# The rebiased weight word goes to a PSUM bank: a three-step weight unpacking in front of a split-precision MLP

## The chip, the cores and the metric

The kernel runs on one core of a Trainium2 chip. The metric is device time in microseconds, taken as the median over repeated executions. A core has TensorE (PE in the profile; PEld is its weight load), VectorE (DVE), ScalarE (ACT), GpSimd (POOL) and SyncE (SP, which issues most of the transfers). They share an SBUF; matmuls write to PSUM, which this kernel uses as eight banks of 128 x 512 words.

## The reference

```python
# q, k, v: [4, 8, 576, 64]; up-local attention, factor 4
q_d, k_d, v_d = (t.reshape(B, H, 144, 4, D).mean(axis=3) for t in (q, k, v))
out_up = np.repeat(sm_attn(q_d, k_d, v_d), 4, axis=2)       # pooled attention
mask = np.abs(pos[:, None] - pos[None, :]) < 4              # band of 7 keys
scores = np.where(mask, scale * q @ k.T, -1e9)
out_local = softmax(scores) @ v
x = (out_up + out_local).transpose(0, 2, 1, 3).reshape(2304, 512)
h = x @ w_in;  x = (h - np.tanh(h)) @ w_out                 # first MLP, 512 -> 2048 -> 512
h = x @ w_in2; return (h * np.cos(h)) @ w_out2              # second MLP
```

The weights come as float64, so the kernel reads each as two 32-bit words.

## The kernel before, in words

**Chunks.** The tokens go through the first MLP in six chunks: batch 0 (512 columns), two halves of batch 1 (256 columns each, the second and the third chunk), batch 2, batch 3 (512 each), and the remaining rows of all batches (256). While one chunk is in the MLP, the attention of the next ones is worked out. After that the second MLP runs.

**Attention.** The band of seven keys is computed by products on POOL (`prod_s` L551 for scores, `prod_v` L600 for values, 128 x 896 each) and sums on DVE (L556, L604), with the softmax between them. The pooled attention uses TensorE (scores `pa_s`, transposes `pa_t`, values `pa_v`). `fin_t` transposes the result into a PSUM tile `pa_x`, `fin_add` adds the pooled part (L642) and makes the high half `xh` (ACT), and `fin_lo` makes the low half `xl` (L653, DVE). A chunk's first-layer matmuls (L742) need `xh` and `xl` of all four head pairs.

**The first MLP.** Every product is computed as three matmuls of high and low halves: wh·xh, wh·xl, wl·xh. L742 is the first layer; ACT's tanh and DVE's L786 make g = h - tanh h, which ACT (L753) and DVE (L788) split into `gh` and `gl`; L762 is the second layer, into four accumulators.

**The weights.** Class `Weights` brings the 32 tiles of one MLP (128 x 512 each, 16 of w_in called `i`, 16 of w_out called `o`) into halves. `load` fetches the two words into a tile `raw` (SP). `begin` runs two ACT instructions: L120 rebiases the exponent of the high word from `raw` into a tile `wf`, L122 prepares the low word inside `raw`. `mid` merges the two on DVE (L126: shift `wf` left by three, or with the word in `raw`, back into `wf`), and makes the high half `hi` from `wf` (L132 on POOL for the first three tiles, ACT L134 for the others). `end` makes the low half (L141 on POOL, `wf` minus `hi`). `tick` does, for one tile, `mid`, the `load` of a later one into the `raw` that came free, the `begin` of the next tile, and the `end` of the one before. SP issues its transfers in one row: the loads of `raw`, and those of `qt`, `kt`, `vt` for the attention.

**What sets the order.** Up to program time 41 (about 48 us in the trace) the instructions run as they are written. Behind that, a scheduler orders them by its own simulated timeline and by priorities; the written times (`add_events`, `pos`) only say when work is offered. Each engine then runs its instructions strictly in its row. PSUM has two banks called `h` (pool `ps_h`, hidden layer), two called `a` (`ps_a`, everything that the attention puts into PSUM), and four others, which are the attention's (`ps_1`, `ps_w`) at first and the accumulators' from program time 41.

Of the kernel before, what the change touches and what calls it, by code (L numbers as in the profile page):

```python
# [8 lines left out]
F32 = mybir.dt.float32  # L9
F32R = mybir.dt.float32r  # L10
AF = mybir.ActivationFunctionType
# [16 lines left out]
def kernel(  # L28
# [11 lines left out]
    nc = tc.nc  # L40
# [15 lines left out]
    U32, U16 = mybir.dt.uint32, mybir.dt.uint16  # L56
    PS = bass.MemoryType.PSUM

    def pool(name, bufs=1, **kw):
        return tc.tile_pool(name=name, bufs=bufs, **kw)  # L60
# [5 lines left out]
    ps_h = ctx.enter_context(pool("ps_h", 2, space=PS))  # L66
    ps_a = ctx.enter_context(pool("ps_a", 2, space=PS))
# [9 lines left out]
    wts_b = []  # L77
# [4 lines left out]
    class Weights:  # L82
# [27 lines left out]
        def begin(self):  # L110
            if self.begun == len(self.order):
                return
            r2, = self.tmp[self.begun]
            wd = wst.tile([128, 512], F32, tag="wf", name="wf", bufs=3)
            r4 = r2.rearrange("p c w -> p (c w)").bitcast(U16).rearrange("p (c w) -> p c w", w=4)
            self.tmp[self.begun] += [wd, r4]
            self.begun += 1


            nc.scalar.activation(wd, r2[:, :, 1].bitcast(F32), AF.Prelu, scale=2.0 ** -112, alpha=-2.0 ** 32)  # L120

            nc.scalar.activation(r2[:, :, 0], r4[:, :, 1], AF.Copy, scale=2.0 ** -13, bias=-0.5 + 2.0 ** -14)  # L122

        def mid(self):
            r2, wd, r4 = self.tmp[self.mids]
            nc.vector.scalar_tensor_tensor(out=wd.bitcast(U32), in0=wd.bitcast(U32), scalar=3, in1=r2[:, :, 0],  # L126
                                           op0=ALU.logical_shift_left, op1=ALU.bitwise_or)
            kind, f = self.order[self.mids]
            pl = w2e if self is W2 and self.mids < NE else wts if f < KA else wts_b[0]
            hi, lo = pl.tile([128, 2, 512], F32R, tag=f"{kind}{f}", name=f"{kind}{f}").rearrange("p a c -> a p c")  # L130
            if self is W1 and self.mids < 3:
                nc.gpsimd.tensor_copy(hi, wd)  # L132
            else:
                nc.scalar.activation(hi, wd, AF.Copy)  # L134
            self.hi[kind, f], self.lo[kind, f] = hi, lo
            self.mids += 1

        def end(self, eng):
            r2, wd, r4 = self.tmp.pop(self.done)
            kind, f = self.order[self.done]  # L140
            eng.tensor_tensor(out=self.lo[kind, f], in0=wd, in1=self.hi[kind, f].bitcast(F32), op=ALU.subtract)  # L141
            self.done += 1

        def tick(self, rawp, eng):

            if self.done == len(self.order):
                return
            if self.mids < len(self.order):
                if self.begun == self.mids:
                    self.begin()  # L150
                self.mid()
                self.load(rawp)
                if self.begun < self.loaded:
                    self.begin()
            if self.mids > self.done + 1 or self.mids == len(self.order):
                self.end(eng)
# [651 lines left out]
    W1, W2 = Weights(w_in1, w_out1), Weights(w_in2, w_out2)  # L808
# [169 lines left out]
```

## Time and profile before

| | |
|---|---|
| median of 3 executions | 949.79 us (948.58 to 951.3) |
| profiled execution, span from first to last instruction | 946.1 us |
| mean granted TensorE clock in it | 0.983 |
| busy share of the span: PE, PEld, DVE, ACT, POOL | 96%, 79%, 64%, 51%, 44% |
| chain that ended last, by engine | PE 68%, DVE 12%, ACT 6%, DMA 5%, POOL 4% |

The span is that of one profiled execution. The median lies 3.7 us above it; that is taken for what lies around a span in an execution. Times in rows are microseconds from the start of the span. The busy shares are averages over stages that differ much: the attention ends early, the second MLP has PE almost alone.

### The profile page before, as it was taken

To read this page: it belongs to the slowest core of one execution; us is meant where nothing else is said; L and a number is where in the kernel's file an instruction comes from. 1 tells how busy PE (TensorE), PEld (TensorE's weight loads), DVE (VectorE), ACT (ScalarE), POOL (GpSimd) and SP (SyncE) were. 2 spreads that over 40 slices of the span, in tenths; PEclk is the share of its full clock that TensorE was granted. 3 is DMA by queue.
4 is the path that set the end of the run, shared out by engine and by line. 5 is a ranking of instruction groups with operands and counts; after the bars stand their busy time and mean duration, and the time that the engine had idled before them with its cause. 6 is when DMAs were issued, how large, how long until landed. Compare 5 with 4: busy or idle time off the path is not lost.

```text
span 946.1 us, 13554 instructions
## 1 busy us (share of the span) xinstructions
PE 904.2 (96%) x4930; PEld 747.6 (79%) x4930; DVE 602.0 (64%) x964; ACT 479.3 (51%) x1012; POOL 413.7 (44%) x432
## 2 busy tenths in 40 slices
PE   7869989999998999999999989999999999999995
PEld 4547757899997777778889968888888888888894
DVE  6599898899989873762236486545645553654453
ACT  3559767333433343383238886445544453544453
POOL 3578988889888983630005543111111110111110
PEclk9978989999999999999999999999999999999998
DMA  9688635532322222181024631010101010100100
GB/s 180 127 287 283 196 113 165 161 99 82 103 85 92 82 66 63 55 254 37 1 89 138 216 114 45 1 45 1 45 1 45 5 41 0 45 23 1 45 1 23
DMA packets 65819, 81.73 MB, mean 86 GB/s; under 512 B 21846, under 2 KB 46428, under 8 KB 65752
## 3 DMA queue, kind: packets, MB, share of 16 engines
q1 hardware_dynamic: 64520, 76.14, 27.0%
q0 software_dynamic: 1232, 4.72, 1.5%
q8 instruction: 39, 0.64, 0.3%
q14 instruction: 28, 0.23, 0.1%
HBM read 71.40 MB, written 9.44 MB: 85 GB/s over the span
## 4 chain that ended last, share of the span: by engine, by line
PE 68%; DVE 12%; ACT 6%; DMA 5%; POOL 4%; issue 3%; SPq 0%; ACTq 0%; DVEq 0%; POOLq 0%
PE h L742 32%; PE oacc L899 21%; PE acc L762 12%; DVE wf L126 3%; DMA raw<-in_moe_w_out_dram 2%; POOL pr L600 2%; DVE s L556 1%; DMA raw<-in_moe_w_in_dram 1%; DMA vt<-in_v_dram 1%; POOL pr L551 1%; ACT raw L122 1%; DMA qt<-in_q_dram 1%; ACT wf L120 1%; DVE h L786 1%; DVE o L604 1%
## 5 line engine op out<-in xcount | busy, mean ns | idle before, releaser
L899 PE MATMUL oacc<-o,i 128*128 128x512 f32 x864 | 209.8, 392 | 3.3 <-ACT i L749 2.8
L742 PE MATMUL h<-xh,i 128*128 128x512 f32 (+1 forms) x768 | 207.7, 346 | 4.2 <-DVE gl L788 4.2
L762 PE MATMUL acc<-gh,o 128*128 128x512 f32 (+1 forms) x768 | 197.9, 339 | 5.7 <-ACT gh L753 5.6
L742 PE MATMUL h<-x2h,i 128*128 128x512 f32 (+1 forms) x640 | 193.2, 369 | 0.0
L899 PEld LDWEIGHTS oacc<-o,i 128*128 128x128 f32 x864 | 160.8, 188 | 39.2 <-ACT i L749 4.0
L914 POOL TENSOR_SCALAR y<-y 128x512 f32<-128x512 f32 (+1 forms) x80 | 47.4, 593 | 327.5 <-ACT y L912 322.2
L742 PEld LDWEIGHTS h<-xh,i 128*128 128x128 f32 x768 | 137.0, 194 | 22.2 <-DVE gl L788 4.9
L762 PEld LDWEIGHTS acc<-gh,o 128*128 128x128 f32 x768 | 132.7, 190 | 23.3 <-ACT gh L753 7.7
L742 PE MATMUL h<-xl,i 128*128 128x512 f32 (+1 forms) x384 | 133.3, 348 | 3.8 <-DVE xl L500 2.8
L742 PEld LDWEIGHTS h<-x2h,i 128*128 128x128 f32 x640 | 116.8, 188 | 21.7
L551 POOL TENSOR_TENSOR pr<-qt,kt 128x896 f32<-128x896 f32 x56 | 120.8, 2171 | 28.1 <-DVE o L604 19.4
L762 PE MATMUL acc<-gl,o 128*128 128x512 f32 (+1 forms) x384 | 129.1, 339 | 0.0
L742 PE MATMUL h<-x2l,i 128*128 128x512 f32 (+1 forms) x320 | 117.9, 369 | 0.0
L600 POOL TENSOR_TENSOR pr<-vt,s 128x896 f32<-128x896 f32 x56 | 107.4, 1964 | 4.1 <-issue 1.7
L919 DVE TENSOR_TENSOR h<-h,rr 128x512 f32<-128x512 f32 (+1 forms) x80 | 51.6, 645 | 83.3 <-ACT rr L918 83.1
L917 ACT ACTIVATE rr<-rr 128x512 f32<-128x512 f32 (+1 forms) x80 | 47.1, 589 | 103.4 <-DVE rr L916 103.4
L742 PEld LDWEIGHTS h<-xl,i 128*128 128x128 f32 x384 | 74.5, 194 | 12.6 <-DVE xl L500 3.5
L921 DVE TENSOR_TENSOR i<-h,i 128x512 fp32r<-128x512 f32 (+1 forms) x80 | 50.6, 634 | 48.7 <-ACT i L749 48.5
L762 PEld LDWEIGHTS acc<-gl,o 128*128 128x128 f32 x384 | 72.8, 190 | 8.2 <-issue 0.4
L126 DVE SCALAR_TENSOR_TENSOR wf<-wf,raw 128x512 uint32<-128x512 uint32 x64 | 64.4, 1015 | 21.7 <-ACT wf L120 15.1
L785 ACT ACTIVATE th<-h 128x512 f32<-128x512 f32 x72 | 42.7, 594 | 67.8 <-PE h L742 67.7
L753 ACT ACTIVATE gh<-h 128x512 fp32r<-128x512 f32 x72 | 42.8, 595 | 65.9 <-PE acc L762 45.1
(184 smaller groups left out, 1264.9 us busy)
## 6 DMA issues: line engine op xcount, KB each, us to landing
raw<-in_moe_w_in_dram SPq DMA_DIRECT2D x32, 512.0 KB
raw<-in_moe_w_out_dram SPq DMA_DIRECT2D x32, 512.0 KB
kt<-in_k_dram SPq DMA_DIRECT2D x16, 320.0 KB
vt<-in_v_dram SPq DMA_DIRECT2D x16, 320.0 KB
out_dram<-os SPq DMA_DIRECT2D x18, 256.0 KB
kt<-in_k_dram SPq DMA_DIRECT2D x16, 256.0 KB
vt<-in_v_dram SPq DMA_DIRECT2D x16, 256.0 KB
x2l<-x2d POOLq DMA_DIRECT2D x4, 1024.0 KB, 5.7
```

Of the source, the lines that this page charges most:

```text
L126: nc.vector.scalar_tensor_tensor(out=wd.bitcast(U32), in0=wd.bitcast(U32), scalar=3, in1=r2[:, :, 0], op0=ALU.logical_shift_left, op1=ALU. ...
L551: nc.gpsimd.tensor_tensor(out=pr.rearrange("p j f d -> p j (f d)"), in0=view(L["q", h], [[0, OFF], [1, 2 * D]], off=f * D), in1=view(L["k" ...
L600: nc.gpsimd.tensor_tensor(out=pr.rearrange("p f d j -> p j f d"), in0=view(L["v", h], [[D, OFF], [D, 2], [1, D]], off=f * D), in1=view(L[" ...
L742: nc.tensor.matmul(hp[:, i * n:i * n + n], lhsT=wt[:, kk * 128:(kk + 1) * 128], rhs=xt, start=(c == 0), stop=(c == 3 * KD - 1))
L753: nc.scalar.activation(gh, hp, AF.Copy)
L762: nc.tensor.matmul(acc[e], lhsT=wt[:, e * 128:(e + 1) * 128], rhs=gt, start=(f == 0 and i == 0), stop=(f == KF - 1 and i == 2))
L785: it = nc.scalar.activation(th, hp, AF.Tanh)
L899: nc.tensor.matmul(acc[t], lhsT=gt[:, t * 128:(t + 1) * 128], rhs=wt, start=(g == 0 and a_ == 0), stop=(g == KF - 1 and a_ == 2))
L914: ip = nc.gpsimd.tensor_scalar(out=y, in0=y, scalar1=-ROUND, scalar2=-TWO_PI_HI, op0=ALU.add, op1=ALU.mult)
L917: nc.scalar.activation(r, r, AF.Abs)
L919: nc.vector.tensor_tensor(out=hp, in0=hp, in1=r, op=ALU.mult)
L921: nc.vector.tensor_tensor(out=G[f][1], in0=hp, in1=G[f][0].bitcast(F32), op=ALU.subtract)
```

## The change

For the first MLP, `begin` writes the rebiased word no longer to `wf` but to a PSUM tile `wp`. It takes this tile from the rotation `h` for the tiles unpacked up to program time 41 (six of them), and from the rotation `a` for the other 26. The merge reads `wp` and `raw` and writes `wf`. The step that begins the next tile right behind a merge is dropped for the first MLP, so that a tile is begun in the step that merges it. The second MLP's weights are unpacked as before. From here on the changed program's lines stand four lower than the same lines of before (L126 is L130, L653 is L657).

```diff
@@ def begin(self):
             wd = wst.tile([128, 512], F32, tag="wf", name="wf", bufs=3)
             r4 = r2.rearrange("p c w -> p (c w)").bitcast(U16).rearrange("p (c w) -> p c w", w=4)
-            self.tmp[self.begun] += [wd, r4]
+            pre = wd
+            if self is W1:
+                bank = (ps_a, "a") if wts_b else (ps_h, "h")
+                pre = bank[0].tile([128, 512], F32, tag=bank[1], name="wp")
+            self.tmp[self.begun] += [wd, r4, pre]
             self.begun += 1
-            nc.scalar.activation(wd, r2[:, :, 1].bitcast(F32), AF.Prelu, scale=2.0 ** -112, alpha=-2.0 ** 32)
+            nc.scalar.activation(pre, r2[:, :, 1].bitcast(F32), AF.Prelu, scale=2.0 ** -112, alpha=-2.0 ** 32)
             nc.scalar.activation(r2[:, :, 0], r4[:, :, 1], AF.Copy, scale=2.0 ** -13, bias=-0.5 + 2.0 ** -14)
@@ def mid(self):
-            r2, wd, r4 = self.tmp[self.mids]
-            nc.vector.scalar_tensor_tensor(out=wd.bitcast(U32), in0=wd.bitcast(U32), scalar=3, in1=r2[:, :, 0],
+            r2, wd, r4, pre = self.tmp[self.mids]
+            nc.vector.scalar_tensor_tensor(out=wd.bitcast(U32), in0=pre.bitcast(U32), scalar=3, in1=r2[:, :, 0],
                                            op0=ALU.logical_shift_left, op1=ALU.bitwise_or)
@@ def tick(self, rawp, eng):
                 self.mid()
                 self.load(rawp)
-                if self.begun < self.loaded:
+                if self.begun < self.loaded and self is not W1:
                     self.begin()
```

How the rows move is seen at two places. The first is ACT's row at the first weight tiles, in the part that runs as written. Before, the second tile (L120 and L122) is begun right behind the first:

```order
L120 ACTIVATE wf_627<-raw_214 128x512
L122 ACTIVATE raw_214<-raw_214 128x512
L120 ACTIVATE wf_635<-raw_216 128x512
L122 ACTIVATE raw_216<-raw_216 128x512
L302 ACTIVATE pt_642<-pa_t_638 128x320
L480 ACTIVATE cp_645<-cpt_646 70x512
L325 ACTIVATE up0_131<-pa_v_664 128x128
L326 ACTIVATE up_l2_99<-pa_v_664 128x32
L311 ACTIVATE pe_554<-pa_t2_678 16x320
```

Now the same place on ACT reads so, in the changed program's lines:

```order
L124 ACTIVATE wp_628<-raw_214 128x512
L126 ACTIVATE raw_214<-raw_214 128x512
L306 ACTIVATE pt_640<-pa_t_636 128x320
L484 ACTIVATE cp_643<-cpt_644 70x512
L329 ACTIVATE up0_131<-pa_v_662 128x128
L330 ACTIVATE up_l2_99<-pa_v_662 128x32
L315 ACTIVATE pe_554<-pa_t2_676 16x320
L124 ACTIVATE wp_683<-raw_216 128x512
L126 ACTIVATE raw_216<-raw_216 128x512
```

The second tile's two instructions went behind five of the attention.

The second place is DVE's row where chunk 0's last hidden tile is done and the second chunk's input is finished. `xl` here is the second chunk's, `pa_x` and `up` its transposed result and its pooled part; L604 sums value products of the third chunk, and L556 score products of batch 2. Before:

```order
L788 TENSOR_TENSOR gl_2079<-h_2062,gh_2078 128x512
L604 TENSOR_REDUCE o_1967<-pr_1968 128x2x64
L642 TENSOR_TENSOR pa_x_2120<-pa_x_2120,up_1751 128x256
L604 TENSOR_REDUCE o_1967<-pr_1988 128x2x64
L642 TENSOR_TENSOR pa_x_2123<-pa_x_2123,up_1939 128x256
L588 RECIPROCAL r_1963<-r_1963 128x4
L653 TENSOR_TENSOR xl_2102<-pa_x_2120,xh_2101 128x256
L625 TENSOR_REDUCE vd_2438<-vt_2199 128x64
L653 TENSOR_TENSOR xl_2102<-pa_x_2123,xh_2101 128x256
L604 TENSOR_REDUCE o_2011<-pr_2012 128x2x64
```

Now, from the first score sum of batch 2 (L560) to the second chunk's last `xl` (L657):

```order
L560 TENSOR_REDUCE s_2228<-pr_2229 128x7x2
L646 TENSOR_TENSOR pa_x_2126<-pa_x_2126,up_1240 128x256
L560 TENSOR_REDUCE s_2228<-pr_2237 128x7x2
L657 TENSOR_TENSOR xl_2134<-pa_x_2126,xh_2133 128x256
...
L560 TENSOR_REDUCE s_2228<-pr_2244 128x7x2
...
L560 TENSOR_REDUCE s_2228<-pr_2283 128x7x2
L657 TENSOR_TENSOR xl_2134<-pa_x_2152,xh_2133 128x256
L646 TENSOR_TENSOR pa_x_2155<-pa_x_2155,up_1971 128x256
L560 TENSOR_REDUCE s_2286<-pr_2287 128x7x2
L570 TENSOR_REDUCE m_2294<-s_2228 128x8
L657 TENSOR_TENSOR xl_2134<-pa_x_2155,xh_2133 128x256
```

Before, the last `xl` of the second chunk stood ahead of every score sum of batch 2; now it stands behind five of them. POOL's row has its products in the same order as before.

## Rows read from the trace of the kernel before

**Rows 1.** The page's part 1: busy time of each engine over the span.

```profile
PE 904.2 (96%) x4930; PEld 747.6 (79%) x4930; DVE 602.0 (64%) x964; ACT 479.3 (51%) x1012; POOL 413.7 (44%) x432
```

**Rows 2.** Stretches: length; busy (count) PE, PEld, DVE, ACT, POOL; clock; DMA share, GB/s.

```profile
120.00:130.00 10.00, 6.96 (x29) 4.80 (x27) 9.82 (x12) 7.61 (x20) 8.33 (x10) 0.94 0.27 85
130.00:140.00 10.00, 10.00 (x39) 6.93 (x38) 8.81 (x8) 6.35 (x12) 9.86 (x6) 0.72 0.32 96
60.00:160.00 100.00, 90.48 (x395) 69.12 (x391) 91.11 (x124) 77.08 (x177) 91.90 (x80) 0.88 0.65 210
...
192.00:300.00 108.00, 106.98 (x850) 101.22 (x851) 97.54 (x152) 42.33 (x118) 94.16 (x78) 1.00 0.30 92
```

**Rows 3.** The merge L126, 40 to 165 us: shortest, median, longest (ns).

```profile
L126 DVE SCALAR_TENSOR_TENSOR wf<-wf,raw x32: 675/1210/2607, 44.3 to 156.4; 128x512 uint32<-128x512 uint32 x32
```

**Rows 4.** The hidden layer's L788 on DVE, same stretch, same columns.

```profile
L788 DVE TENSOR_TENSOR gl<-h,gh x13: 654/678/692, 80.4 to 160.5; 128x512 fp32r<-128x512 f32 x13
```

**Rows 5.** Groups by shape, 60 to 160 us: busy us, mean ns | idle before.

```profile
L126 DVE SCALAR_TENSOR_TENSOR wf<-wf,raw 128x512 uint32<-128x512 uint32 x28 | 35.6, 1282 | 2.6 <-ACT wf L120 2.5
...
L551 POOL TENSOR_TENSOR pr<-qt,kt 128x896 f32<-128x896 f32 x12 | 27.6, 2306 | 1.9 <-DMA kt<-in_k_dram 1.3 <-DVE s L556 0.5
L141 POOL TENSOR_TENSOR o<-wf,o 128x512 fp32r<-128x512 f32 x16 | 22.4, 1405 | 1.0 <-ACT o L134 1.0
L141 POOL TENSOR_TENSOR i<-wf,i 128x512 fp32r<-128x512 f32 x13 | 18.4, 1414 | 1.8 <-ACT i L134 1.6
L600 POOL TENSOR_TENSOR pr<-vt,s 128x896 f32<-128x896 f32 x8 | 16.8, 2134 | 0.1
L560 POOL TENSOR_TENSOR s<-s,mask_t 128x28 f32<-128x28 f32 x6 | 3.2, 532 | 2.4 <-DVE s L556 2.4
L260 POOL COPY qz<-klq 64x64 f32<-64x64 f32 x8 | 2.8, 351 | 0.2
```

**Rows 6.** POOL groups by shape, 190 to 300 us, where no merge runs.

```profile
L551 POOL TENSOR_TENSOR pr<-qt,kt 128x896 f32<-128x896 f32 x25 | 52.7, 2125 | 5.4 <-DVE s L556 3.3 <-DVE o L604 1.8 <-DVE pr__2362 L279 0.2
L600 POOL TENSOR_TENSOR pr<-vt,s 128x896 f32<-128x896 f32 x20 | 37.3, 1929 | 0.4 <-DVE s L556 0.2
L260 POOL COPY qz<-klq 64x64 f32<-64x64 f32 x8 | 1.9, 233 | 0.3
L560 POOL TENSOR_TENSOR s<-s,mask_t 128x56 f32<-128x56 f32 x6 | 1.9, 309 | 2.7 <-DVE s L556 2.7
```

**Rows 7.** Timeline around one merge, DVE: start, duration, instruction.

```profile
115.33 1.92 DVE L126 SCALAR_TENSOR_TENSOR wf<-wf,raw 128x512 uint32<-128x512 uint32 x1
```

**Rows 8.** Timeline there, POOL.

```profile
116.67 1.74 POOL L141 TENSOR_TENSOR i<-wf,i 128x512 fp32r<-128x512 f32 x1
...
118.80 1.29 POOL L141 TENSOR_TENSOR o<-wf,o 128x512 fp32r<-128x512 f32 x1
```

**Rows 9.** DVE's timeline, 176 to 200 us, [idle before <- releaser].

```profile
185.40 0.41 DVE L653 TENSOR_TENSOR xl<-pa_x,xh 128x256 fp32r<-128x256 f32 x1
...
199.91 1.07 DVE L556 TENSOR_REDUCE s<-pr 128x14 f32<-128x896 f32 x1
```

**Rows 10.** POOL's timeline, 176 to 204 us.

```profile
191.56 0.52 POOL L260 COPY qz<-klq 64x64 f32<-64x64 f32 x2
...
197.36 2.13 POOL L551 TENSOR_TENSOR pr<-qt,kt 128x896 f32<-128x896 f32 x1 [0.65 <-DVE s L556]
```

**Rows 11.** PE's timeline around the second chunk's start.

```profile
185.87 0.39 PE L742 MATMUL h<-xl,i 128*128 128x256 f32 x1 [0.82 <-DVE xl L653]
...
190.96 0.73 PE L762 MATMUL acc<-gh,o 128*128 128x256 f32 x4 [0.74 <-ACT gh L753]
```

**Rows 12.** PE's timeline where batch 2 follows.

```profile
303.33 0.50 PE L742 MATMUL h<-xh,i 128*128 128x512 f32 x1 [2.29 <-DVE gl L788]
```

**Rows 13.** Timeline of DVE and SP at the second tile.

```profile
46.17 0.68 DVE L126 SCALAR_TENSOR_TENSOR wf<-wf,raw 128x512 uint32<-128x512 uint32 x1
...
46.88 0.35 SPq L108 DMA_DIRECT2D raw<-in_moe_w_out_dram  x1
```

More of the change, by code (lines that the diff above doesn't have):

```diff
@@ L138, in end @@
         def end(self, eng):
-            r2, wd, r4 = self.tmp.pop(self.done)
+            r2, wd, r4, pre = self.tmp.pop(self.done)
             kind, f = self.order[self.done]
```

## Prediction

> **What bounds the kernel now.** The page's busy shares come first [rows 1]: PE is busy 904.2 us of 946.1, so on the whole the time is PE's, and only two things can change it, PE's idle time and PE's clock. The stretches say where those are [rows 2]. From 192 us on PE is busy in 106.98 of 108 us at full clock: there nothing helps, and whatever shift reaches that point is carried to the end. From 60 to 160 us three engines are nearly full at once: PE 90.48 us of 100, DVE 91.11, POOL 91.90. [...] So the weights' stage, 60 to 160 us, and its handover to the second chunk decide.
>
> Next I look at what the merge costs. Its groups by shape and its spread [rows 3, 5] show 675 ns at the shortest, 1210 at the median and 2607 at the longest, 35.6 us in 28 merges. Another DVE operation of the same size in the same stretch, L788, which reads one operand from PSUM, keeps to 654 to 692 ns in all 13 cases [rows 4]. So the stretch is not hard on DVE as such; it is hard on the operation with both inputs in SBUF. POOL pays as well: the `lo` subtraction that ran beside a merge of 1.92 us took 1.74 us, and the next one, without a merge beside it for most of its length, 1.29 [rows 7, 8].
>
> The handover is the last place to look. The second chunk's last `xl` starts on DVE at 185.40 and takes 0.41 us [rows 9]; PE waits 0.82 us for it at 185.87 [rows 11]. It is the gate of that chunk.
>
> **The change, part by part.** *The merge.* With one operand in PSUM it has the operand places of L788, so I take 0.68 us for it in place of 1282 ns: 28 × 0.60 = 17 us of DVE time come free. The bounds are 0.68 (L788) and 1.28 (no effect). DVE is no bound of its own here, since it stands in turn with POOL; so this does not go into the sum directly. What goes in is what POOL gets.
>
> [...]
>
> *POOL.* I compare group means of 60 to 160 us with those of 190 to 300 us, where no merge runs [rows 5, 6]. Score products: 12 × (2306 - 2125) ns = 2.2 us. Value products: 8 × (2134 - 1929) = 1.6. The `lo` subtractions, against the 1.29 us of one almost alone [rows 8]: 16 × 0.115 + 13 × 0.124 = 3.4. L560: 6 × (532 - 309) = 1.3, where 309 ns is for twice as many elements. L260: 8 × 0.118 = 0.9. About 13 other small operations and two products before 60 us I put at 1.6 by the same proportions (an estimate). Together 11.0 us. At most POOL would gain the merge's whole uncontended length each time, 28 × 0.675 = 19 us; at least nothing.
>
> POOL's 8 us of idle in that stretch [rows 2] are partly waits for DVE (2.4 for L556 [rows 5]) and can shrink when DVE is ahead: I take 2, between 0 and 5.
>
> *The later beginning.* A tile is now begun in its merging step. In the written part the second tile's pair on ACT stands behind five of the attention's instructions, and its merge, 46.17 us before, is that much later; SP's next weight load waits for the `raw` that this merge frees (46.88) [rows 13], and the loads of `qt` and `kt`, POOL's first food, are queued behind it. I charge 1 us (0 to 2, the length of the inserted instructions). Later on each merge waits for its own tile's two ACT instructions; ACT has 23 us of 100 free [rows 2], so I count nothing for it, and price the case that this cover fails as a rival. ACT's write to PSUM shows in no row. It would have to be 0.7 us longer per tile to use up ACT's free 23 us on 32 tiles; I take nothing for it.
>
> So POOL's lane is ahead by S = 11 + 2 - 1 = 12 us at the handover (9 to 16 for this case).
>
> *The handover.* The order shows the thing that speaks against a gain. The second chunk's last `xl` now stands behind five score sums of batch 2 on DVE. DVE runs its row strictly, so the gate is no longer where the second chunk's own transposes are ready, but where POOL has made five more products of 2.1 us. In the times of before, the fifth product starts at 197.36 [rows 10], its sum at 199.91, and after 1.07 us of that sum, an estimated 0.2 for the short maximum behind it and 0.41 for the `xl`, the gate opens at 201.6. The copies, which stand between those products before (0.52 us at 191.56 [rows 10]), stand earlier now, and idles as the 0.65 before the fifth shrink: less 1.6 with their small neighbours, that is 200. With S = 12 the gate opens at 188.0 against 185.8 before: **+2.2 us** (184 to 191, so -1.8 to +5.2).
>
> *PE beside it.* Up to there PE has the same work as before, and gets its weights earlier; what it saves before the gate it loses in front of it as one long idle piece. After 3 us of idle, the stretch of before paid (1 - 0.72) × 10 = 2.8 us at the lower clock [rows 2]. I take **+3** (0 if its waits are split by other matmuls, 3.4 if the lower level lasts as long again). The 0.74 us for `gh` that follow in the second chunk [rows 11] lie behind other work when the two chunks stand closer together: **-1**. The wait of 2.29 us at batch 2's beginning [rows 12] gets a little shorter since POOL and DVE enter it earlier: **-1** (0 to -3.3).
>
> The sum is 2.2 + 3 - 1 - 1 = **+3.2 us**. From 946.1 the span comes to 949.3; with the 3.7 us by which the median lies above the profiled span the time is **953.0 us**.
>
> **The rivals.** *A, the forecast*: the merge is freed, but the handover waits for the five products. For it speaks the order, which is certain, and POOL's load of 91.90 of 100. Own range 949.5 to 956.5 from S of 16 to 9.
>
> *B, faster*: POOL's lane gains so much that the gate opens before PE has its own work done. That takes S above about 16. For it: in that stretch DVE and POOL wait for one another, and a lane gains more than its parts when both get shorter. If S is 20 (19 by the upper bound, 2 regained, 1 lost) the gate opens at 180, and PE is the bound: of its 9.5 us of idle and about 3 of lower clock before that point I give back half, 6, and 1 at batch 2, so 939.1 of span and 942.8 us. Range 939 to 946.9. [...]
>
> *C, slower by more*: two banks `a` carry the attention's PSUM traffic, and 26 tiles now use them too. Each `wp` holds one from ACT's write to the merge's end, some 2 us at least with 0.7 of merge, that is over 50 us of the 200 bank-microseconds of the stretch. Pooled transposes wait for a bank, or DVE stands at a merge whose tile is not begun, and the sums behind it wait. If 7 of the 12 us are lost so, S is 5, the gate opens at 195, and +9.2 + 1 gives 960 (957 to 963 for S of 8 to 2).
>
> *D, the merge is not freed*: the contention goes with something else than the operand's place. S is then 1, the gate opens at 199, +13.2 + 1, and the time is 964. L788's steady 678 ns beside the same POOL operations speak against it.
>
> **How the numbers follow.** A 0.50, B 0.30, C 0.15, D 0.05. Within 0.3%, or 2.85 us, of before (about what a measurement of this kernel can tell from no change) is up to 952.6; nearly half of A lies below that, 0.24. Slower is the rest of A with C and D, 0.46; faster is B, 0.30. Since cases of both signs hold much, the range reaches from inside B to inside C, 941.5 to 961.5, which leaves out about 0.09 below and 0.09 above.
>
> **What would show it.** Right: merges at 0.68 us throughout; L551 at 2.13 and L141 at 1.29 us in 60 to 160 us; POOL's products reaching batch 2 some 12 us earlier; PE idle in front of a first-layer matmul with `xl` as releaser near 188 us, and a lower granted clock behind it. Wrong: merges still above 1 us (D), idle on DVE before L130 or PE waits for banks `a` that add up to more than 5 us (C), or a second chunk that starts before 182 us without a wait for `xl` (B).

## The result and the profile after

The changed kernel takes 963.53 us (961.46 to 965.18, 4 runs) against 949.53 us for the one before: a ratio of 1.0143, with a 95% interval from 1.0124 to 1.0161. It is 14.0 us slower. The prediction had the side right, but its 953.0 us (941.5 to 961.5) lies short of it, and so does the upper end of the range. The profiled execution has a span of 963.3 us, 17.2 more than that of before. Against their own medians the two profiled executions differ by 3 us (0.2 and 3.4 below), so 3 of the 17.2 are differences between executions. Part of them stands at the very start: the first weight tile's ACT instruction, ahead of which the two rows are the same, is at 44.79 us in the changed kernel's trace and at 43.04 in that of before.

The merges first: one instruction's spread over 40 to 175 us, as [rows 3].

```profile
L130 DVE SCALAR_TENSOR_TENSOR wf<-wp,raw x32: 653/682/692, 46.0 to 155.7; 128x512 uint32<-128x512 uint32 x32
```

All 32 run in 653 to 692 ns. The same groups by shape as [rows 5], 60 to 160 us:

```profile
L130 DVE SCALAR_TENSOR_TENSOR wf<-wp,raw 128x512 uint32<-128x512 uint32 x29 | 19.5, 682 | 10.0 <-ACT wp L124 5.0 <-POOL i L145 2.9 <-POOL o L145 1.5
...
L555 POOL TENSOR_TENSOR pr<-qt,kt 128x896 f32<-128x896 f32 x13 | 27.6, 2123 | 0.0
L145 POOL TENSOR_TENSOR o<-wf,o 128x512 fp32r<-128x512 f32 x16 | 20.8, 1298 | 4.2 <-ACT o L138 4.1
L145 POOL TENSOR_TENSOR i<-wf,i 128x512 fp32r<-128x512 f32 x14 | 18.2, 1300 | 0.6 <-ACT i L138 0.4
L604 POOL TENSOR_TENSOR pr<-vt,s 128x896 f32<-128x896 f32 x9 | 17.3, 1954 | 0.1
L564 POOL TENSOR_TENSOR s<-s,mask_t 128x28 f32<-128x28 f32 x7 | 1.8, 254 | 5.9 <-DVE s L560 5.9
L264 POOL COPY qz<-klq 64x64 f32<-64x64 f32 x6 | 1.4, 238 | 0.2
```

POOL's score products take 2123 ns and its `lo` subtractions 1298 and 1300: what they take where no merge runs [rows 6, 8]. The relief is whole. But POOL now idles 5.9 us in one piece for a score sum and 4.1 for `hi` halves, and DVE 10.0 us in front of merges, where it was 2.6 [rows 5]. The start shows where the lateness begins. SP's timeline, in the stretch of [rows 13]:

```profile
50.98 0.35 SPq L108 DMA_DIRECT2D raw<-in_moe_w_out_dram  x1
51.39 0.43 SPq L221 DMA_DIRECT2D qt<-in_q_dram  x1
```

The weight load that stood at 46.88 stands at 50.98, and the load of `qt` behind it. POOL's first product of the third chunk follows at 57.88, where it began at 53.22 before:

```profile
57.88 2.09 POOL L555 TENSOR_TENSOR pr<-qt,kt 128x896 f32<-128x896 f32 x1
```

Rows of ACT say what stood in front of the second tile's pair:

```profile
44.79 0.61 ACT L124 ACTIVATE wp<-raw 128x512 f32<-128x512 f32 x1
...
47.95 0.28 ACT L329 ACTIVATE up<-pa_v 128x128 f32<-128x128 f32 x1 [1.16 <-PE pa_v L326]
...
49.02 0.60 ACT L124 ACTIVATE wp<-raw 128x512 f32<-128x512 f32 x1
```

The first two tiles in the kernel before:

```profile
43.04 0.65 ACT L120 ACTIVATE wf<-raw 128x512 f32<-128x512 f32 x1
...
44.15 0.66 ACT L120 ACTIVATE wf<-raw 128x512 f32<-128x512 f32 x1
```

Of the five instructions, two wait for PE (1.16 us, and 0.38 at the other). The second tile is begun 4.2 us behind the first, where it was 1.1: 3.1 us later. It adds up from tile to tile: the sixth is begun 26.5 us behind the first (at 71.30), where it was 18.4 (at 61.46). PE's timeline shows what that becomes, and the far end of the stage:

```profile
71.55 0.76 PE L746 MATMUL h<-xh,i 128*128 128x512 f32 x1 [6.92 <-ACT xh L500]
...
115.83 0.38 PE L634 MATMUL pa_qk<-ident,qkd 128*128 128x128 f32 x2
...
180.13 0.39 PE L766 MATMUL acc<-gh,o 128*128 128x512 f32 x1
184.58 1.12 PE L298 MATMUL pa_t<-ident,pe 128*128 128x128 f32 x4 [4.06 <-ACT pe L292]
...
202.55 0.74 PE L766 MATMUL acc<-gh,o 128*128 128x256 f32 x4 [1.12 <-ACT gh L757]
204.80 0.55 PE L746 MATMUL h<-xh,i 128*128 128x256 f32 x1 [1.51 <-DVE gl L792]
```

The same places in the kernel before, which were not among its rows shown above:

```profile
64.50 1.23 PE L742 MATMUL h<-xh,i 128*128 128x512 f32 x2
...
80.88 0.68 PE L630 MATMUL pa_qk<-ident,qkd 128*128 128x128 f32 x2
...
182.34 0.39 PE L762 MATMUL acc<-gh,o 128*128 128x512 f32 x1
```

Chunk 0 starts 7 us later and yet ends 2.2 us earlier, so the stage in between gave back 9. (In the trace of the run g3 below, whose rows are the same up to there, chunk 0 starts at 68.98, so of the 7 us some 2.6 can be a difference between executions.) Then PE stands still for 4.06 us and waits for the pooled attention of the second chunk's last head pair, whose transposes (`pa_t`) were done near 155 us before. The second pair's pooled steps began at 115.83 us in place of 80.88. The gate, on POOL and on DVE, as [rows 9, 10]:

```profile
184.36 10.27 POOL L555 TENSOR_TENSOR pr<-qt,kt 128x896 f32<-128x896 f32 x5
```

```profile
195.01 1.08 DVE L560 TENSOR_REDUCE s<-pr 128x14 f32<-128x896 f32 x1
196.00 0.26 DVE L570 TENSOR_REDUCE m<-s 128x8 f32<-128x56 f32 x1
196.17 0.42 DVE L657 TENSOR_TENSOR xl<-pa_x,xh 128x256 fp32r<-128x256 f32 x1
```

The last low half follows the fifth score sum without a gap, at 196.17 instead of 185.40: 10.8 us later. Stretches, with the columns of [rows 2]:

```profile
60.00:70.00 10.00, 4.16 (x61) 3.30 (x58) 6.46 (x12) 3.71 (x7) 6.52 (x4) 0.50 0.33 103
...
180.00:190.00 10.00, 5.23 (x24) 2.52 (x22) 7.56 (x14) 5.20 (x17) 9.65 (x8) 0.69 0.65 215
190.00:200.00 10.00, 8.45 (x49) 8.17 (x49) 9.74 (x18) 2.53 (x8) 10.00 (x8) 0.63 0.42 130
200.00:210.00 10.00, 7.37 (x49) 6.99 (x49) 9.46 (x17) 4.79 (x15) 8.41 (x12) 0.83 0.26 79
...
310.00:337.00 27.00, 23.81 (x105) 18.40 (x104) 21.39 (x35) 10.29 (x28) 22.51 (x21) 0.94 0.23 63
```

PE's granted clock is 0.69, 0.63 and 0.83 of full clock in the three stretches from 180 to 210 us. The second chunk's first wait of its second layer stands 11.6 us later (202.55), the next wait 12.8 (204.80 for 192.01 before), and batch 2's wait of [rows 12] 13.4 (316.75 for 303.33). The remaining 3.8 of the profile's 17.2 us are behind that, partly in lower clock, as the 0.94 from 310 to 337 us (1.00 before, from 297 to 324).

### The profile page after: what moved, and what is told of

Read it like the earlier page. It is cut to its first block, busy times and chain, and to the rows that moved or that the text cites. A ratio compares the mean times of both kernels' runs of the same rounds, so it can differ in the third digit from the quotient of the medians.

```text
span 963.3 us, 13558 instructions
## 1 busy us (share of the span) xinstructions
PE 910.1 (94%) x4922; PEld 753.9 (78%) x4930; DVE 584.0 (61%) x964; ACT 479.2 (50%) x1012; POOL 401.2 (42%) x432
## 3 DMA queue, kind: packets, MB, share of 16 engines
q1 hardware_dynamic: 64520, 76.14, 26.5%
## 4 chain that ended last, share of the span: by engine, by line
PE 71%; DVE 8%; DMA 8%; ACT 5%; POOL 5%; issue 2%; SPq 0%; ACTq 0%; DVEq 0%; POOLq 0%
PE h L746 33%; PE oacc L903 20%; PE acc L766 13%; DMA raw<-in_moe_w_out_dram 3%; DMA raw<-in_moe_w_in_dram 2%; POOL pr L555 2%; POOL pr L604 2%; DVE wf L130 1%; DMA kt<-in_k_dram 1%; ACT raw L126 1%; PE idle L361 1%; DVE s L560 1%; PE pa_s L271 1%; ACT i L138 1%; PE pa_t L298 1%
## 5 line engine op out<-in xcount | busy, mean ns | idle before, releaser
L746 PE MATMUL h<-xh,i 128*128 128x512 f32 (+1 forms) x768 | 209.9, 349 | 11.0 <-ACT xh L500 6.9
L746 PEld LDWEIGHTS h<-xh,i 128*128 128x128 f32 x768 | 139.4, 198 | 29.9 <-issue 9.8
L555 POOL TENSOR_TENSOR pr<-qt,kt 128x896 f32<-128x896 f32 x56 | 117.9, 2120 | 38.9 <-DVE o L608 33.3
L604 POOL TENSOR_TENSOR pr<-vt,s 128x896 f32<-128x896 f32 x56 | 105.8, 1932 | 6.3 <-DVE o L608 4.3
L790 DVE TENSOR_TENSOR h<-h,th 128x512 f32<-128x512 f32 x72 | 49.7, 692 | 59.3 <-ACT th L789 59.3
```

Source lines behind the costliest of these rows:

```text
L555: nc.gpsimd.tensor_tensor(out=pr.rearrange("p j f d -> p j (f d)"), in0=view(L["q", h], [[0, OFF], [1, 2 * D]], off=f * D), in1=view(L["k" ...
L604: nc.gpsimd.tensor_tensor(out=pr.rearrange("p f d j -> p j f d"), in0=view(L["v", h], [[D, OFF], [D, 2], [1, D]], off=f * D), in1=view(L[" ...
L746: nc.tensor.matmul(hp[:, i * n:i * n + n], lhsT=wt[:, kk * 128:(kk + 1) * 128], rhs=xt, start=(c == 0), stop=(c == 3 * KD - 1))
L790: nc.vector.tensor_tensor(out=hp, in0=hp, in1=th, op=ALU.subtract)
```

## The experiments

Three theories were put to the test. A: the beginning in the merging step is what costs. B: the attention's pooled steps and the weight tiles hold each other up in the two banks `a`. C: the five score sums ahead of the last low half set the second chunk's start. Changed lines are given against the changed kernel, or against the kernel before where that is said. Times are medians, with the ratio to the kernel before and its 95% interval; each set is compared with the kernel before, on the same chip, at 949.8 to 950.7 us. A start can differ by 1 to 3 us between two traces, so a shift of that size between two traces is not read as an effect.

**Beginning late without PSUM**, and the same for the six tiles of the written part only. Both are the kernel before with one condition:

```diff
-                if self.begun < self.loaded:
+                if self.begun < self.loaded and self is not W1:                # e2
+                if self.begun < self.loaded and (self is not W1 or wts_b):     # g2
```

> The merge from SBUF as before; only the beginning ahead is dropped for the first MLP. Theory A (the later beginning): in the written part the first score product on POOL slips from 53.2 us to about 57.5, the first layer of chunk 0 by some 7 us, merges stay at a median near 1.2 us, so nothing is given back: 954 to 958 us. Theory B (the two banks of the attention tie its pooled steps to the weights): no bank is shared here, pooled steps of the last head pair stay near 150 us, and the time stays at 949 to 952 us. Theory C (five score sums in front of the last low half): the order of the handover is that of before, so as B.

> The kernel before (rebiased word in SBUF), with the beginning ahead dropped for the six tiles of the written part alone. If the 14 us of the run that dropped it everywhere come from the start: 957 to 965 us and the first layer at 70 us instead of 64.5. If they come from the 26 tiles behind the written part: 949 to 953 us.

They took 964.94 us (ratio 1.0150, 1.0135 to 1.0165) and 964.56 (1.0159, 1.0133 to 1.0184). So beginning late costs 14 to 15 us by itself, and all of it comes from six tiles in the written part: with these six late, the other 26 add nothing that shows. That is more than the 954 to 958 that theory A expected of the first. PE's timeline of the first of them:

```profile
74.93 0.80 PE L742 MATMUL h<-xl,i 128*128 128x512 f32 x1 [3.36 <-DVE xl L500]
86.19 1.92 PE L762 MATMUL acc<-gh,o 128*128 128x512 f32 x4 [3.13 <-ACT gh L753]
```

The first layer's low half is 6.4 us later than in the kernel before (68.50), and the second layer's start 7.3 later (86.19 for 78.91), with a wait of 3.13 us in front of it in place of 1.83. The last matmul of chunk 0 stands at 194.51, 12.2 us later than the 182.34 of before, so most of the 14 us is lost by the end of chunk 0. Why the 7 us grow to 12 inside it stays open.

**PSUM with the beginning ahead kept**, everywhere or in the written part only:

```diff
-                if self.begun < self.loaded and self is not W1:
+                if self.begun < self.loaded:                                       # e1
+                if self.begun < self.loaded and (self is not W1 or not wts_b):     # e3
```

> The change with the beginning ahead kept everywhere, so that only the place of the rebiased word differs from before. Theory A: as the run before, 949 to 955 us. Theory B: a tile begun ahead holds its bank longer, so the pooled steps come no earlier than with the change: 960 to 966 us. Theory C: six sums ahead of the last low half, gate 2 us later than in the run before.

> The change with the beginning ahead kept in the written part only. Theory A: the 7 us of the start come back, POOL keeps its shorter operations, the gate of the second chunk opens near 189 us: 949 to 955 us. Theory B: the start is early, but the pooled steps of the last head pair still stand behind weight tiles in the two banks, later than 165 us; PE waits in front of the second chunk and falls to the lower clock: 957 to 963 us. Theory C: the order has four score sums ahead of the last low half; gate at about 188 us by POOL alone, 952 to 956 us.

956.39 us (1.0062, 1.0037 to 1.0086) and 961.89 (1.0113, 1.0096 to 1.0130). With the beginning ahead everywhere the loss shrinks from 14.0 to 6 us but stays; 956.39 lies neither in A's range nor in B's. The second time lies in B's. Theory A does not explain what is left, and B was wrong in expecting the tiles held longer to cost more: it is the other way round, by 5.5 us. So in PSUM it is above all the 26 later tiles whose late beginning costs: 5.5 us, against 1.6 for the six (961.89 for 963.53, with intervals that touch). The first of the two is the best look at the change's two sides. POOL's and PE's timelines:

```profile
171.47 3.47 POOL L604 TENSOR_TENSOR pr<-vt,s 128x896 f32<-128x896 f32 x2
```

```profile
168.93 0.39 PE L766 MATMUL acc<-gh,o 128*128 128x512 f32 x1
...
171.09 1.01 PE L271 MATMUL pa_s<-kT,qz 128*128 128x144 f32 x6 [0.57 <-issue]
180.43 1.11 PE L298 MATMUL pa_t<-ident,pe 128*128 128x128 f32 x4 [8.33 <-ACT pe L292]
```

POOL ends the third chunk's value products at 174.9 us, where it did at 187.6 before: 12.7 us ahead. PE ends chunk 0 at 169.3, where it did at 182.7: 13.4 ahead. And then PE waits 8.33 us for the last pair's pooled steps, whose scores come at 171.09 (144.78 before), at the end of which the second chunk starts later than before.

**The hidden layer's banks for all tiles**, with the beginning late as in the change:

```diff
-                bank = (ps_a, "a") if wts_b else (ps_h, "h")
+                bank = (ps_h, "h")
```

> The change with all 32 tiles in the two banks of the hidden layer, none in the attention's. Theory A: the start is as late as with the change, 961 to 965 us. Theory B: the pooled steps are free again (last head pair before 160 us), but now chunk 0's hidden tiles stand between weight tiles in their banks, PE waits inside chunk 0, and the time is 965 us or more. Theory C: seven sums ahead of the last low half, so 963 us or more.

978.96 us (1.0299, 1.0281 to 1.0318). As theory B expected (C's "963 us or more" is met too), the cost moves: PE's waits in 60 to 190 us are now led by the second layer's, for the hidden tiles' `gh`:

```profile
PE acc L766 <- ACT gh L757: 11.5, 6, 3.7
```

**Weights' steps written further apart** (one number, `TW` from 1.4 to 2.6), so that the last pairs' pooled steps come between weight tiles in the banks' rotation: with PSUM and beginning ahead (f3), in the kernel before (f5), and in the change itself (f4).

```diff
-    TS, TS_POOL, TW = 2.5, 0.9, 1.4
+    TS, TS_POOL, TW = 2.5, 0.9, 2.6
```

> As the run with the beginning ahead kept everywhere and the rebiased word in PSUM, but the weights' steps are written 2.6 instead of 1.4 time units apart (one number), so that in program order the last two head pairs' pooled steps stand among the weight tiles in the rotation of the two banks and not behind all of them. Theory B (rotation in program order): the last pair's pooled values come before 165 us in place of 182, PE does not idle for it at the end of chunk 0, the second chunk starts near 172 us, and POOL's gain of 12 us reaches the end: 934 to 944 us. Theory C (sums of batch 2 ahead of the last low half are what counts): 950 to 956 us. A theory that the spread itself makes weights late: over 957 us.

> Control: the kernel before with the same one number (2.6), the rebiased word in SBUF. If the number helps only by freeing the two banks, nothing is gained here: 947 to 953 us. If the order of weights against attention is worth something by itself, it shows here as under 946 or over 954 us.

> The change as it is (begun in the merging step) with the same one number (2.6). Theory B with the later beginning as a cost of its own: pooled steps free as in the first of these runs, the start 7 us later, so 6 to 12 us more than that run: 943 to 953 us. If beginning late costs nothing where banks are free: the same as that run.

959.16 us (1.0077, 1.0046 to 1.0107), 951.83 (1.0014, 1.0001 to 1.0027), and 953.62 (1.0038, 1.0023 to 1.0053). The first missed theory B's range by 15 us or more and lies where weights made late were expected. The last pair's pooled values do come earlier (175.00 for 182.37 in the run without the spread), but the merges now run until late:

```profile
L130 DVE SCALAR_TENSOR_TENSOR wf<-wp,raw x32: 672/691/701, 45.4 to 176.2; 128x512 uint32<-128x512 uint32 x32
```

The last merge starts at 176.2, where it did at 153.1 in the run without the spread. The pooled values are 7.4 us earlier and the last merge 23.1 later; that the weight tiles now wait for the pooled ones, and so the banks hold up whichever stands second, is read from these two times. The control shows that the number does little by itself. In the change, begun late as it is, it gives back 9.9 of the 14.0 us: the last pair's values come at 173.45 in place of 186.52, and PE no longer stands still for them at the end of chunk 0.

```profile
173.45 0.49 PE L323 MATMUL pa_v<-pt,vd 128*64 128x160 f32 x4
```

The last low half (188.35) is there ahead of every score sum of batch 2 (the first at 188.68), so this run takes away what theory B and what theory C names, and does not part them. That it is 5.5 us faster than the run that begins ahead is against theory A; the two intervals overlap, and it is not explained. In the slower one two sums still stand ahead of the last low half, and PE waits 1.66 and 2.59 us for `gh` and `gl` after 195 us, in the faster one 0.75 for `gl`.

**A bank of their own.** From the run with the beginning ahead everywhere: one of the two banks goes to the weight tiles, the other to the attention, until the second chunk starts.

```diff
-    ps_a = ctx.enter_context(pool("ps_a", 2, space=PS))
+    ps_a = ctx.enter_context(pool("ps_a", space=PS))
+    alt = [0, 0]
+    def ta():
+        if wts_b and not alt[1]:
+            return "a0"
+        alt[0] ^= 1
+        return f"a{alt[0]}"
...                     (every other tile of ps_a takes its tag from ta(); alt[1] counts the chunks)
-                bank = (ps_a, "a") if wts_b else (ps_h, "h")
+                bank = (ps_a, "a1") if wts_b else (ps_h, "h")
```

> PSUM and beginning ahead everywhere, written times as before; one of the two banks goes to the weight tiles alone, the other to the attention alone, until the second chunk starts. Theory B: no attention tile stands behind a weight tile; but pooled steps have one bank and go one by one. The last pair's pooled values near 170 us by the order: better than with shared banks (956), 942 to 954 us.

959.07 us (1.0087, 1.0068 to 1.0107), a miss: with a single bank the pooled steps are slow in themselves. The first pair's steps are early again, at 63.07, where they stood at 75.71 in the run with shared banks (e1); but the last pair's values come at 178.51 us.

```profile
63.07 0.64 PE L642 MATMUL pa_qk<-ident,qkd 128*128 128x128 f32 x2
...
177.13 0.59 PE L306 MATMUL pa_t<-ident,pe 128*16 128x128 f32 x2 [2.15 <-ACT pt L314]
```

PE waits 2.15 us for ACT to read the pair's first transposes before the second ones can go to the one bank.

**Fewer tiles in PSUM**, beginning ahead everywhere: six (the written part, hidden layer's banks) and ten (four of them in banks `a`).

```diff
-            if self is W1:
+            if self is W1 and not wts_b:          # e7
+            if self is W1 and self.begun < 10:    # g1
```

> PSUM for the six tiles of the written part alone (in the hidden layer's two banks, idle there), beginning ahead everywhere; the 26 others as before. Theory B: no bank of the attention is touched in the weights' stage, so no loss: 946 to 951 us. If PSUM's place by itself costs something: over 953 us.

> PSUM for the first ten tiles, beginning ahead everywhere. In program order the four tiles behind the written part stand ahead of every pooled step of the second chunk. Theory B by program order: pooled steps wait for those four tiles only, a start of the first pair later by some 10 us, 949 to 954 us; if the start of the pooled chain is what counts and not its last pair: over 954 us.

948.92 us (0.9989, 0.9976 to 1.0002) and 959.54 (1.0100, 1.0071 to 1.0130). PSUM by itself costs nothing that shows; four tiles in the attention's banks cost 10 us, more than the 26 of e1, which free the later merges too. In that run the pooled chain starts its first pair late, and every later pair with it:

```profile
77.54 0.38 PE L634 MATMUL pa_qk<-ident,qkd 128*128 128x128 f32 x2
...
106.29 0.44 PE L634 MATMUL pa_qk<-ident,qkd 128*128 128x128 f32 x2
...
160.87 0.44 PE L634 MATMUL pa_qk<-ident,qkd 128*128 128x128 f32 x2
```

Before, these stand at 61.46, 80.88 and 139.03 us. The four pairs form one chain of 20 to 30 us a pair, and 16 us at its start are 22 at its end, although no later tile is in these banks.

**The sums held back.** The change (g3), and PSUM with the beginning ahead (h1), with batch 2's first sums behind the second chunk's last low half:

```diff
-            nc.vector.tensor_tensor(out=ch.x[1][:, u, :], in0=a, in1=ch.x[0][:, u, :].bitcast(F32), op=ALU.subtract)
+            ch.last = nc.vector.tensor_tensor(out=ch.x[1][:, u, :], in0=a, in1=ch.x[0][:, u, :].bitcast(F32), op=ALU.subtract).ins
@@ def red_s(u, e, f, pr):
+            with ExitStack() as st:
+                if ch is chunks1[3] and u < 2:
+                    st.enter_context(tc.issue_after(chunks1[1].last))
...                     (the sum itself, now inside the `with`)
```

> The change, with batch 2's score sums of its first two head pairs held on DVE until the second chunk's last low half is issued, so that the five sums no longer stand ahead of it. Theory C (the sums set the gate): the last low half comes at 189 to 192 us in place of 196.2 and the time falls by 4 to 7 us, 956 to 960 us. Theory B (the pooled steps, late by the two banks, set it): POOL is only stopped for longer, the gate opens at 193 us or later by the transposes, 961 to 966 us.

> PSUM with the beginning ahead everywhere (956.4 us) and batch 2's sums held behind the last low half, as in the run that held them for the change itself (956.9 for 963.5). If late beginning and sums are two costs that add: 949 to 951 us. If PE, already idle for 8 us in front of the last pair's transposes, is bound by the pooled steps alone here: 954 to 957 us.

956.89 us (1.0074, 1.0048 to 1.0100) and 952.54 (1.0020, 1.0007 to 1.0033). In the change the last low half comes at 190.84 in place of 196.17, and 6.6 us are gained, as theory C expected. Of these 5.3 us in the traces, 3.3 are a difference between executions: g3's rows are the same as the change's until the sums, and its POOL ends the third chunk's value products at 181.19 where the change's does at 184.49. The sums move the low half by 2.0; behind it, PE's waits of 1.12 and 1.51 us become none and 0.23. With the beginning ahead 3.9 are gained (known to about 2.6 only, as e1's times spread from 952.57 to 961.93), between the 5.4 to 7.4 of costs that add and the 2.4 at most of pooled steps alone. PE still waits 6.09 us for the last pair there. The gate in g3, then that wait in h1:

```profile
190.84 0.42 DVE L660 TENSOR_TENSOR xl<-pa_x,xh 128x256 fp32r<-128x256 f32 x1 [0.45 <-ACT xh L656]
191.18 2.07 DVE L563 TENSOR_REDUCE s<-pr 128x14 f32<-128x896 f32 x2
```

```profile
178.40 1.11 PE L298 MATMUL pa_t<-ident,pe 128*128 128x128 f32 x4 [6.09 <-ACT pe L292]
```

**The accumulators' banks** for the tiles begun before chunk 0's second layer, with the others from SBUF as before and the beginning ahead (h6), and the same with the sums held back as above (h7):

```diff
-            if self is W1:
-                bank = (ps_a, "a") if wts_b else (ps_h, "h")
+            if self is W1 and not acc_on:
+                bank = (ps_acc, "acc") if wts_b else (ps_h, "h")
...                     (acc_on is an empty list at first)
@@ def ffn1(...):
             if j == 2:
+                acc_on.append(1)
```

> PSUM for the tiles begun before chunk 0's second layer starts: six in the hidden layer's banks, about eleven in the four banks of the accumulators, not in the attention's; the others from SBUF as before; beginning ahead everywhere. Banks of the attention as the cause of the loss: the pooled steps of the last pair stay near 150 to 165 us, no loss, and about half of POOL's relief is kept: 943 to 949 us. If any PSUM use of the tiles costs, or the accumulators start late: over 953 us.

> The run before with batch 2's sums held behind the last low half. If the sums are a cost wherever they stand ahead: 2 to 6 us less than that run. If the second chunk's start is there set by PE: the same.

960.48 us (1.0093, 1.0066 to 1.0121) and 959.77 (1.0086, 1.0056 to 1.0117), not the 943 to 949 us hoped for; accumulators that start late were the alternative named. The pooled steps stay early (the last pair's values at 166 us), but the accumulators stand behind weight tiles in their banks in program order, and chunk 0's second layer starts at 94.92 us where it did at 78.91:

```profile
94.44 0.69 PE L299 MATMUL pa_t<-ident,pe 128*128 128x128 f32 x2 [4.12 <-ACT pe L293]
94.92 0.80 PE L767 MATMUL acc<-gh,o 128*128 128x512 f32 x1
```

Holding the sums back makes no difference there, as was expected if PE sets the second chunk's start. No version was faster than the kernel before by more than its runs can tell.

## Why the prediction was wrong

The side came right, and with it the gate behind the five sums, from which the forecast's +3 came. The size did not: what made 14.0 us of it stood in the sum at 1 us and at nothing. Two steps failed, the later beginning and the cover for the banks.

*The merge* was right: 682 ns taken for 0.68 us, with the spread gone. The merges with a PSUM operand have a median of 682 ns, and the shortest from SBUF alone was 675 [rows 3].

*POOL* was right: 11 us from shorter operations and 2 of idle were counted, and with the beginning kept ahead POOL stands 12.7 us ahead at the end of the third chunk. Rival D is out, and so is B, which needed a lead above 16; the 19 us estimated as the most that POOL could gain were not reached.

*The later beginning* failed first. Two terms stood for it: "I charge 1 us (0 to 2, the length of the inserted instructions)" for the written part, and "so I count nothing for it" for the tiles behind. The inserted instructions' own length is 1.9 us, but two of them wait for PE, and the delay grows from 3.1 us at the second tile to about 8 at the sixth. POOL's last value products of the third chunk, in the kernel before, in the change, in g3 (the same rows up to there) and in e3, show what S became:

```profile
183.95 3.64 POOL L600 TENSOR_TENSOR pr<-vt,s 128x896 f32<-128x896 f32 x2
...
181.00 3.49 POOL L604 TENSOR_TENSOR pr<-vt,s 128x896 f32<-128x896 f32 x2
...
177.70 3.49 POOL L607 TENSOR_TENSOR pr<-vt,s 128x896 f32<-128x896 f32 x2
...
176.75 3.51 POOL L604 TENSOR_TENSOR pr<-vt,s 128x896 f32<-128x896 f32 x2
```

They end at 187.6, 184.5, 181.2 and 180.3. So S was 12.7 with the beginning ahead everywhere (e1), 7.3 with it ahead in the written part alone (e3), and in the change 3.1 by its own trace and 6.4 by g3's, where 12 was forecast. Beginning late takes 6 to 10 us of S and not 1, and some 5 of that belong to the 26 tiles for which nothing was counted. In time it costs 7.1 us beside PSUM (963.53 for e1's 956.39), and 14.7 alone (g2).

*The handover* was right in its mechanism: the gate opens behind the fifth sum, and the gap between POOL's fifth product and the last low half is as worked out (194.6 to 196.6, 2 us). Its time, 196.6 in place of 188.0, follows from S: the forecast's own 200 less 3.1 gives 196.9. The sums are worth 6.6 us (g3). By the same sum A's own range, for S of 16 to 9, is 949.0 to 956.0 and not 949.5 to 956.5; nothing hangs on it.

*The cover for banks* failed second. C named the mechanism, "two banks `a` carry the attention's PSUM traffic", and DVE that stands at a merge whose tile is not begun. Its own sign came: more than 5 us of idle on DVE before L130 (10.0, of which 5.0 for ACT's `wp`; e1 has 8.7 as well, so part of it is room that DVE gained). Its S of 5 and its gate at 195 are close to what the change shows, and 963.5 lies just above its 957 to 963; it was given 0.15. What C had not is the second way in which the banks cost. With the beginning ahead they take nothing from POOL (S is 12.7 in e1), but they make the pooled chain late. In the kernel before that chain had over 20 us of room in front of the gate (last pair's values at 162 us, gate at 185.8). In e1 PE waits 8.33 us for the last pair's transposes, and the kernel loses 6 us with S whole. In the change the pooled chain is the last to arrive but one: the fifth sum comes 2 us after it.

*PE beside it*: +3 for the lower clock. In after, PE's granted clock is 0.69, 0.63 and 0.83 in the three stretches from 180 to 210 us (0.50, the lower level, throughout 184 to 196). Weighted by its busy time that is, as an estimate, 5.23 × 0.31 + 8.45 × 0.37 + 7.37 × 0.17 = 6.0 us, of which only about 2 lie behind the gate's own 10.8 (12.8 at 204.80). The two terms of -1 did not come: the waits there are 1.12 us for 0.74, and 2.25 and 0.94 at batch 2 for 1.01 and 2.29.

The costs do not add: late beginning 14.7, PSUM 6, both 14.0. Four runs say what the 14.0 consist of. Of the change's 14.0 us, 7.1 are left with the sums held back (g3), 6.0 with the beginning ahead (e1), and 1.8 with both (h1, 1.0007 to 1.0033). So the late beginning and the sums together make 12.2 of the 14.0. What is left is 1.8 us, and POOL's 12.7, which do not reach the end. The late pooled chain, for which PE still waits 6.09 us in h1, goes with that; that it is this chain alone is not shown.

What stays open is why the six tiles' late beginning costs 14.7 us alone and hardly anything beside PSUM, where the 26 others' costs 5.5; no run begins only the 26 late from SBUF, so it is not shown that the shared banks make this difference. Open, too, is why the change with the weights' steps spread (f4) is no slower than the same with the beginning ahead (f3).

## What to carry to other kernels

When an operand moves to PSUM, list who takes tiles from the same banks in program order, and ask of each how much room it has: the one that had room may be last to arrive afterwards, though nothing about its own instructions has changed. When a pair of instructions is moved behind others on an engine that runs its row strictly (here ACT stood idle for 1.16 us in front of L329, with the second tile's pair behind it), count the waits of what stands ahead as well as their lengths, and follow the delay over all the tiles that repeat it (3.1 us at the second, about 8 at the sixth here). And a relief that is real, 12.7 us on the busiest lane here, is worth nothing until the next lane to arrive at the same gate is known. Two traces of the same rows differ by 3 us here before anything has been changed; such a shift is to be taken off before a row's time is read as an effect.

## What was not expected of the hardware

In the changed kernel the merge with one operand in PSUM kept to 653 to 692 ns beside a POOL busy for 86.35 us of 100 (60 to 160 us), and the POOL operations there to what they take where no merge runs (score products 2123 ns, `lo` subtractions 1298 and 1300); with both in SBUF the same merge took up to 2607 ns [rows 3]. The prediction had taken this from other operations' rows; that it holds for all 32 merges is what these runs add. What was not expected is that a lower clock lasted far longer than in the 10 us of [rows 2]: with 4.06 us of idle at the start and a run of short waits behind it (1.12 and 1.51 us among them), the granted clock was 0.69, 0.63 and 0.83 in three stretches of 10 us.
